# Linear attention with an MLP: where the second token tile's keys and queries stand in a planned instruction order

## The chip, the cores and the metric

The kernel runs on one core of one Trainium2 chip. Its time is the device time of one execution in microseconds (us), given as the median of several runs. The engines are named as in the profile: PE (TensorE, its matmuls; PEld its weight loads), DVE (VectorE), ACT (ScalarE), POOL (GpSimd) and SP (SyncE, whose queue issues every DMA here).

## The reference, cut to what matters

For 8 batches, 8 heads, 576 tokens and a head size of 64, queries and keys are scaled, projected by `omega` to 128 features, shifted by a maximum and exponentiated. Keys and values are summed into a state for each batch and head, queries read it, and the result goes through a layer norm and an MLP of width 2048.

```python
def phi(x):
    proj = np.einsum('bhsd,md->bhsm', x, omega)
    sq = np.sum(x * x, axis=-1, keepdims=True) / 2.0
    h = proj - sq
    h = h - np.max(h, axis=-1, keepdims=True)
    return np.exp(h) / np.sqrt(m)
q_p, k_p = (phi(q_s), phi(k_s))
kv = np.einsum('bhsm,bhsd->bhmd', k_p, v)
z = np.sum(k_p, axis=2)
num = np.einsum('bhsm,bhmd->bhsd', q_p, kv)
den = np.einsum('bhsm,bhm->bhs', q_p, z)[..., None] + 1e-06
...
x = (num / den).transpose(0, 2, 1, 3).reshape(B, S, H * D)
xn = (x - mu) / np.sqrt(var + 1e-06) * g_ln
out = x + np.maximum(xn @ w_ch1, 0.0) @ w_ch2
```

The term `sq` falls out against the maximum, so the kernel never computes it. Here `q` is drawn 4.742 times as large as `k`.

## The kernel before

**Tiles of tokens.** The 4608 tokens are 9 tiles of 512. A tile is 2 query blocks of 256, or 4 chunks of 128. The MLP takes tile after tile (`gen_mlp`): for each of 16 slices f of the hidden width, `mm1(t, f)` is 12 matmuls of 512 columns (L797 to L799: 4 slices of the model width, each with a high and a low part of the weights and of the data) and `mm2(t, f)` 12 more (L830 to L832). `mm2(t, f)` stands behind `mm1(t, f + 1)`. `mm1(t, f)` waits for the group of four first-layer weights that holds f (`w(1, 4*(f//4)+k)`), `mm2(t, f)` for `w(2, f)`.

**Weights.** The 32 weight parts come as 64-bit numbers. `gen_w` loads each one with a 512 KB DMA (L343), turns it into 32-bit numbers with steps on DVE and ACT (L352 to L368), and splits it into a high and a low part. The last step is L379 for first-layer weights and L385 for second-layer ones. At most 3 conversions are open at a time (`turn["w"]`), each with one of 14 `wide` buffers.

**Keys.** `gen_keys` goes through batches b and chunks c of 128 tokens; a batch has 4, and one chunk more holds the remainders of two batches. `gen_k` loads keys and values (L426, L427), projects the keys with 8 unsplit matmuls on 64-row tiles (L514; the trace shows 16 records for them), takes maxima on DVE (L445), exponentiates on ACT (L451), sums into the state on PE (`sums`, L483) and adds it up on DVE (`keep`, L499).

**Queries.** There are two ways. `gen_q`, used for the first tile (`blk < T // QB`, blocks 0 and 1), loads `qT` (L544) and projects it unsplit with 4 matmuls of 256 columns on 64-row tiles (L554; 8 records), two heads side by side. `gen_q2`, used for every other block, loads `qD` (L575), in which each head's numbers stand twice on the partitions, rounds it on ACT (L580), subtracts on DVE to get the low part (L582), and projects with two matmuls of 512 columns against a high and a low `omega` (L589, L590). A block takes 2 calls of `gen_q` or 4 of `gen_q2`. Then `features` copies from PSUM (L230 or L232), takes the maximum over partitions on POOL (L611), subtracts on DVE (L614) and exponentiates on ACT (L617).

**From queries to the MLP.** `gen_x` multiplies the query features of a chunk with the state (L680), divides on DVE (L691 to L695) and takes mean and variance (L713, L715). `gen_rs` makes the reciprocal root for a block (L726 to L738). `gen_xnT` normalizes (L756) and transposes on PE (L770); ACT and DVE write the two parts of `xnT` (L774, L776). There is one `xnT` buffer: the next tile's is written after the last `mm1` of the tile before.

**PSUM.** Of 8 banks, the MLP has 6 once it runs (`mlp_on`); keys, queries, products and transposes share the other two (`at_now`).

**The order.** All instructions are put in order beforehand by a planner in Python (`Plan`), which keeps a clock per engine and a cost per step (the numbers in `us(...)`, `act`, `dve`). Of the steps that can start on an engine it takes the one with the lowest `rank`; MLP steps have the rank `LAST`, so they fill what is left. A `yield wait(...)` or a turn only shapes this order. In the program that comes out, an instruction waits for the data and buffers it uses, and each engine and the SP queue work in the planned order. Ranks before:

- weights: first layer -12 to -10.5 for f below 4, then f - 13.5; second layer f - 10;
- key chunk c of batch 1: 2 + 2c; queries of blocks 2 and 3: 10 and 14; their products and statistics 6 to 8 above;
- `GATE_K`, `GATE_Q`: keys of batch 1 and later enter the plan once `w(2, 5)` is converted, queries of block 2 and later once `w(2, 6)` is.

Tile 1 (the second tile, tokens 512 to 1023) needs the state of batches 0 and 1, so the four chunks of batch 1, and query blocks 2 and 3.

Of the kernel before, what the change touches and what calls it, by code (L numbers as in the profile page):

```python
# [19 lines left out]
PE, ACT, DVE, POOL, SP = "PE", "ACT", "DVE", "POOL", "SP"  # L20
# [15 lines left out]
T = 512  # L36
# [3 lines left out]
QB = 256  # L40
# [28 lines left out]
class Plan:  # L69
# [73 lines left out]
    def free(self, *names):  # L143
        for n in names:
            assert n not in self.places, n
            self.places[n] = self.cur.seen()
            self.cur.holds -= n[0] == "b" and 0 < self.cur.holds
            self.wake(lambda w: w[0] == "get" and n in w[1])

    def done(self, key):  # L150
        self.made[key] = self.cur.seen()
        self.wake(lambda w: w == ("wait", key))
# [38 lines left out]
def favor_ffn(ctx, tc, kT, kTr, vF, vR, qT, qD, omT, gT, w1, w2, out):  # L191
# [21 lines left out]
    def f32(ap):  # L213
        return ap.bitcast(F32)
# [4 lines left out]
    def dve(n, k=1, c=0.065):  # L219
        return "run", {DVE: k * (c + 0.00105 * n)}  # L220

    def us(eng, t):
        return "run", {eng: t}

    def dma(n):
        return "run", {SP: n * 4e-6 / 0.36}
# [13 lines left out]
    def wait(*key):  # L240
        return "wait", key
# [4 lines left out]
    def tile_of(tag, shape, dtype=F32, pool=None):  # L246
        pool = pool or (wp if tag[1].isdigit() and tag[0] == "w" else small if tag[0:2] in ("kv", "mb", "st") or tag[0] == "v" else sb)
        return pool.tile(shape, dtype, tag=tag, name=tag, bufs=1)
# [6 lines left out]
    def bank(tag, n=512):  # L255
        return tile_of(tag, [P, 512], F32, ps)[:, 0:n]
# [10 lines left out]
    mlp_on = []  # L267

    def at_now():
        return b_at if mlp_on else banks  # L270
# [152 lines left out]
    def gen_k(b, c, kraw, v, early, t_v, n_kp):  # L423
# [19 lines left out]
        def side(s, t_b, pk):  # L443
            yield dve(4 * M)
            nc.vector.tensor_reduce(  # L445
                out=mb[:, 4 * s : 4 * s + 4], in_=pk, axis=AX.X, op=ALU.max, negate=True
            )
            yield act(M, 4, 0.142)
            for i in range(4):
                j = 4 * s + i  # L450
                nc.scalar.activation(  # L451
                    out=kp[:, j], in_=pk[:, i], func=AF.Exp, scale=1.0, bias=mb[:, j : j + 1]
                )
            free(t_b)
            done(("kp", b, c, s))
# [50 lines left out]
        plan.add(rank, values())  # L506
        if TILED:
            t_b = yield "get", at_now(), 2
            yield us(PE, 0.9)
            pk = [bank(x).rearrange("p (a b) -> p a b", b=M) for x in t_b]  # L510
            for p in range(NP):
                for h in range(2):
                    a = slice(h * D, (h + 1) * D)
                    nc.tensor.matmul(pk[h][:, p], kraw[a, p], om[a], start=True, stop=True)  # L514
            for s in range(2):
                plan.add(rank, side(s, t_b[s], pk[s]))
        else:
            for s in range(2):
                t_b = yield "get", at_now()
                yield us(PE, 0.87)  # L520
                pk = bank(t_b).rearrange("p (a b) -> p a b", b=M)
                for p in range(2):
                    nc.tensor.matmul(
                        pk[:, 2 * p : 2 * p + 2], kraw[:, 2 * s + p], om, start=True, stop=True
                    )
                plan.add(rank, side(s, t_b, pk))
# [10 lines left out]
    def gen_q(blk, j):  # L537
        rank = plan.cur.rank
        first = n_first if blk < T // QB else ()
        q_turn = () if first else ((yield "get", turn["q"]),)  # L540
        t_q = yield "get", first + n_big
        qraw = tile_of(t_q, [P, 2, QB])
        yield dma(P * 2 * QB)
        nc.sync.dma_start(qraw, qT[blk, j])  # L544
        yield wait("om")

        if TILED:
            t_b = yield "get", at_now(), 2
            yield us(PE, 0.87)
            pq = [bank(x) for x in t_b]  # L550
            for p in range(2):
                for h in range(2):
                    a = slice(h * D, (h + 1) * D)
                    nc.tensor.matmul(pq[h][:, p * QB : (p + 1) * QB], om[a], qraw[a, p], start=True, stop=True)  # L554
            for s in range(2):
                plan.add(rank, features(blk, j, s, t_b[s], pq[s]))
        else:
            for s in range(2):
                t_b = yield "get", at_now()
                yield us(PE, 0.87)  # L560
                pq = bank(t_b)
                for h in range(2):
                    nc.tensor.matmul(pq[:, h * QB : (h + 1) * QB], om[:, h], qraw[:, s], start=True, stop=True)
                plan.add(rank, features(blk, j, s, t_b, pq))
        free(t_q, *q_turn)
# [3 lines left out]
    def gen_q2(blk, j, s):  # L569
        rank = plan.cur.rank  # L570
        q_turn = yield "get", turn["q"]
        t_q = yield "get", n_big
        qraw = tile_of(t_q, [P, 2 * QB])
        yield dma(P * 2 * QB)
        nc.sync.dma_start(qraw, qD[blk, j, s].rearrange("p a b -> p (a b)"))  # L575
        yield wait("om2")
        t_s = yield "get", n_big
        qs = tile_of(t_s, [P, 2 * QB], F32R)
        yield act(2 * QB)
        nc.scalar.copy(out=qs, in_=qraw)  # L580
        yield us(DVE, 0.85)
        nc.vector.tensor_tensor(out=qs[D:P], in0=qraw[D:P], in1=f32(qs[D:P]), op=ALU.subtract)  # L582
        free(t_q, q_turn)
        t_b = yield "get", at_now()

        plan.cur.after = max(plan.cur.after, plan.cur.end + LATE)
        yield us(PE, 0.46)
        pq = bank(t_b)
        nc.tensor.matmul(pq, om_hi, qs, start=True, stop=False)  # L589
        nc.tensor.matmul(pq, om_lo, qs, start=False, stop=True)  # L590
        free(t_s)
        yield from features(blk, j, s, t_b, pq)

    def gen_om2():
        yield dve(M)
        nc.vector.tensor_copy(om_hi, om)
        yield dve(M)
        nc.vector.tensor_tensor(out=om_lo, in0=om, in1=f32(om_hi), op=ALU.subtract)
        done(("om2",))

    def features(blk, j, s, t_b, pq):
        t_c = yield "get", n_big
        qc = tile_of(t_c, [P, 2 * QB])
        eng = yield "run", {ACT: 0.48, DVE: 0.62} if blk >= T // QB else {ACT: 0.58}
        copy(eng, qc, pq)
        free(t_b)
        mx_turn = yield "get", turn["mx"]
        t_m = yield "get", n_big
        mx = tile_of(t_m, [P, 2 * QB])
        yield us(POOL, 1.9)  # L610
        nc.gpsimd.partition_all_reduce(mx, qc, P, bass_isa.ReduceOp.max)  # L611
        done(("mx", blk, j, s))
        yield us(DVE, 0.95 if blk >= T // QB else 0.6)
        nc.vector.tensor_tensor(out=qc, in0=qc, in1=mx, op=ALU.subtract)  # L614
        free(t_m, mx_turn)
        yield act(2 * QB)
        nc.scalar.activation(out=qc, in_=qc, func=AF.Exp)  # L617
        phis[blk, j, s] = t_c, qc.rearrange("p (a b) -> p a b", b=QB)
        done(("phi", blk, j, s))
# [6 lines left out]
    def gen_queries():  # L626
        for blk in range(NB):
            if blk == T // QB:
                yield wait("w", 2, GATE_Q)
                plan.add(plan.cur.rank, gen_om2())  # L630
            plan.cur.rank = NS * (blk * QB // T) + RQ + 4 * (blk % 2) - (7 if blk < T // QB else 0)
            b_turn = yield "get", turn["blk"]
            plan.add(plan.cur.rank, gen_block(blk, b_turn))

    def gen_block(blk, b_turn):
        rank = plan.cur.rank
        for j in range(2):
            if blk < T // QB:
                plan.add(rank, gen_q(blk, j))
            else:  # L640
                for s in range(2):
                    plan.add(rank, gen_q2(blk, j, s))
        t_st = yield "get", n_st
        st = tile_of(t_st, [P, 64])
        for i in range(2):
            plan.add(rank + 6 + 2 * i, gen_x(2 * blk + i, t_st, st))
        plan.add(rank + 8, gen_rs(blk, t_st, st))
        for j in range(2):
            for s in range(2):
                yield wait("phi", blk, j, s)  # L650
        yield wait("num", 2 * blk)
        yield wait("num", 2 * blk + 1)
        free(*(phis[blk, j, s][0] for j in range(2) for s in range(2)), b_turn)
# [241 lines left out]
FIRST = 4  # L895
N_BIG = 14
EARLY, BEFORE = 1, ("x", 3)
GATE_K, GATE_Q = 5, 6
LATE = 1.0
WARM, COLD = 0.0, 5.0  # L900
RW, RS = -10, 0.5
RK, RQ = -30, -22


# [37 lines left out]
```

## Time and profile before

| what | value |
|---|---|
| time, median of 3 runs | 1023.02 us (1022.56 to 1023.74) |
| the profiled execution's own time | 1024.08 us |
| its span, first to last instruction | 1022.3 us |
| busy: DVE, ACT, POOL | 500.2, 351.2, 135.3 us |
| mean granted TensorE clock | 0.992 |
| MLP matmuls | 6 groups of 576, mean 390 to 403 ns each |
| first `mm1` of tile 0, of tile 1, of tile 2 begins | 50.76, 175.81, 305.35 us |
| DMA | 64.19 MB, mean 63 GB/s |

A matmul's duration in the profile holds its whole passage through the array; matmuls follow each other more closely than that, so the pace is read from the starts. Windows of the profile count the busy time of each engine between two times; a timeline shows instructions in order, merged when they are alike, with the engine's idle time and the releaser in brackets.

### The profile page before, as it was taken

How to read it: one execution, taken by the hardware profiler on the slowest of the kernel's cores; microseconds unless marked ns; L12 is line 12 of the kernel's file. 1: busy time of each engine (PE TensorE's matmuls, PEld its weight loads, DVE VectorE, ACT ScalarE, POOL GpSimd, SP SyncE). 2: the span in 40 equal slices, each digit the busy share in tenths (PEclk: the TensorE clock that was granted, in tenths of full speed). 3: DMA queues.
4: the chain of work that ended last, by engine and by line, in shares of the span. 5: the costliest groups of instructions: out<-in, count | busy, mean ns of one | idle time of the engine just before them, and what ended most of it. 6: DMA issues, size and time to landing. Idle time of an engine off the chain costs nothing.

```text
span 1022.3 us, 16484 instructions
## 1 busy us (share of the span) xinstructions
PE 1009.1 (99%) x6778; PEld 818.1 (80%) x6778; DVE 500.2 (49%) x1057; ACT 351.2 (34%) x798; POOL 135.3 (13%) x80
## 2 busy tenths in 40 slices
PE   9999997999999999999999999999999999999998
PEld 7888775878778877887888778888888888888886
DVE  6999848537456532574137532661375134113112
ACT  6689743524533522253114421331133111111100
POOL 5000322203202300050002200140022000000000
PEclk9999996999999999999999999999999999999999
DMA  9553313121222210310013100300030010001001
GB/s 351 214 186 140 105 63 111 45 74 63 63 73 85 63 53 1 125 63 22 1 68 119 32 12 1 105 20 1 10 115 1 1 42 1 1 1 43 1 1 41
DMA packets 30315, 64.19 MB, mean 63 GB/s; under 512 B 3488, under 2 KB 3616, under 8 KB 30240
## 3 DMA queue, kind: packets, MB, share of 16 engines
q1 hardware_dynamic: 30240, 63.14, 18.2%
q8 instruction: 53, 0.87, 0.4%
q14 instruction: 22, 0.18, 0.1%
HBM read 53.69 MB, written 9.44 MB: 62 GB/s over the span
## 4 chain that ended last, share of the span: by engine, by line
PE 93%; DVE 3%; DMA 2%; SPq 0%; issue 0%; ACT 0%; DVEq 0%
PE b L830 14%; PE b L797 14%; PE b L799 13%; PE b L798 13%; PE b L831 13%; PE b L832 13%; PE b L514 3%; PE b L483 3%; PE b L680 3%; DMA w<-w 2%; PE b L770 1%; PE b L589 1%; PE b L590 1%; DMA w<-vF 1%; DVE x L841 1%
## 5 line engine op out<-in xcount | busy, mean ns | idle before, releaser
L810 DVE SCALAR_TENSOR_TENSOR hid<-b,hid 128x512 fp32r<-128x512 f32 x144 | 99.4, 690 | 371.8 <-ACT hid L808 371.4
L808 ACT ACTIVATE hid<-b 128x512 fp32r<-128x512 f32 x144 | 86.2, 598 | 434.6 <-PE b L799 433.7
L830 PE MATMUL b<-w,hid 128*128 128x512 f32 x576 | 232.3, 403 | 0.0
L797 PE MATMUL b<-xnT,w 128*128 128x512 f32 x576 | 229.7, 399 | 0.8 <-ACT xnT L774 0.8
L799 PE MATMUL b<-xnT,w 128*128 128x512 f32 x576 | 224.8, 390 | 0.1
L798 PE MATMUL b<-xnT,w 128*128 128x512 f32 x576 | 224.9, 390 | 0.0
L831 PE MATMUL b<-w,hid 128*128 128x512 f32 x576 | 224.8, 390 | 0.0
L832 PE MATMUL b<-w,hid 128*128 128x512 f32 x576 | 224.8, 390 | 0.0
L611 POOL PARTITION_ALL_REDUCE wide<-wide x72 | 134.2, 1893 | 644.1 <-ACT wide L230 589.4
L797 PEld LDWEIGHTS b<-xnT,w 128*128 128x128 f32 x576 | 108.3, 188 | 25.9 <-ACT xnT L774 1.2
L830 PEld LDWEIGHTS b<-w,hid 128*128 128x128 f32 x576 | 108.1, 188 | 25.0
L799 PEld LDWEIGHTS b<-xnT,w 128*128 128x128 f32 x576 | 108.4, 188 | 23.8 <-DVE xnT L776 0.9
L832 PEld LDWEIGHTS b<-w,hid 128*128 128x128 f32 x576 | 108.1, 188 | 23.2
L798 PEld LDWEIGHTS b<-xnT,w 128*128 128x128 f32 x576 | 108.5, 188 | 21.2
L831 PEld LDWEIGHTS b<-w,hid 128*128 128x128 f32 x576 | 108.3, 188 | 20.1
L451 ACT ACTIVATE kp<-b,mb 128x128 f32<-128x128 f32 x272 | 75.1, 385 | 58.9 <-DVE mb L445 58.6
L445 DVE TENSOR_REDUCE mb<-b 128x4 f32<-128x512 f32 x72 | 46.8, 684 | 38.7 <-PE b L514 38.6
L614 DVE TENSOR_TENSOR wide<-wide,wide 128x512 f32<-128x512 f32 x72 | 62.8, 875 | 6.0 <-POOL wide L611 5.5
L617 ACT ACTIVATE wide<-wide 128x512 f32<-128x512 f32 x72 | 45.5, 636 | 42.4 <-DVE wide L614 40.1
L582 DVE TENSOR_TENSOR wide<-wide,wide 64x512 fp32r<-64x512 f32 x64 | 51.5, 806 | 10.1 <-ACT wide L580 8.3
L230 ACT COPY wide<-b 128x512 f32<-128x512 f32 x58 | 33.3, 592 | 54.1 <-PE b L590 49.8
L680 PEld LDWEIGHTS b<-kv,wide 128*64 128x64 f32 (+1 forms) x1088 | 40.7, 140 | 12.1 <-issue 8.1
(70 smaller groups left out, 796.1 us busy)
## 6 DMA issues: line engine op xcount, KB each, us to landing
w<-w SPq DMA_DIRECT2D x32, 512.0 KB, 8.5
wide<-qD SPq DMA_DIRECT2D x64, 256.0 KB, 2.9
out<-x SPq DMA_DIRECT2D x36, 256.0 KB, 2.0
v<-vF SPq DMA_DIRECT2D x28, 260.0 KB, 2.9
wide<-kT SPq DMA_DIRECT2D x28, 256.0 KB, 2.8
w<-vF SPq DMA_DIRECT2D x4, 260.0 KB, 4.9
v<-vR SPq DMA_DIRECT2D x4, 260.0 KB, 4.1
w<-kT SPq DMA_DIRECT2D x4, 256.0 KB, 5.1
```

The source lines that it names most:

```text
L451: nc.scalar.activation(out=kp[:, j], in_=pk[:, i], func=AF.Exp, scale=1.0, bias=mb[:, j : j + 1])
L611: nc.gpsimd.partition_all_reduce(mx, qc, P, bass_isa.ReduceOp.max)
L614: nc.vector.tensor_tensor(out=qc, in0=qc, in1=mx, op=ALU.subtract)
L680: nc.tensor.matmul(pn[a:z, i], phi(blk, h, slice(cols + a, cols + z)), kvs[b][1][:, h], start=True, stop=True)
L797: nc.tensor.matmul(ph, w[:, 0, cs], xnT[:, 0, k], start=(k == 0), stop=False)
L798: nc.tensor.matmul(ph, w[:, 1, cs], xnT[:, 0, k], start=False, stop=False)
L799: nc.tensor.matmul(ph, w[:, 0, cs], xnT[:, 1, k], start=False, stop=(k == NK - 1))
L808: nc.scalar.activation(out=hl[:, 0], in_=ph, func=AF.Relu)
L810: nc.vector.scalar_tensor_tensor(out=hl[:, 1], in0=ph, scalar=0.0, in1=f32(hl[:, 0]), op0=ALU.max, op1=ALU.subtract)
L830: nc.tensor.matmul(accs[i], hl[:, 0, cs], w[:, 0], start=(f == 0), stop=False)
L831: nc.tensor.matmul(accs[i], hl[:, 0, cs], w[:, 1], start=False, stop=False)
L832: nc.tensor.matmul(accs[i], hl[:, 1, cs], w[:, 0], start=False, stop=(f == NF - 1))
```

## The change

Tile 1's queries (blocks 2 and 3) go through `gen_q` instead of `gen_q2` (`WHOLE = 4`), so `qT` holds four blocks and the high and low `omega` are made when block 4 is reached. `GATE_K` and `GATE_Q` fall from 5 and 6 to 3 and 4. The step of the weights' ranks doubles (`RS`), and `RK` and `RQ` fall by 6. The planner's cost of an unsplit projection on 64-row tiles is 1.15 us while the MLP runs, where it was 0.9 for keys and 0.87 for queries.

```diff
@@ gen_k
             t_b = yield "get", at_now(), 2
-            yield us(PE, 0.9)
+            yield us(PE, 1.15 if mlp_on else 0.9)
@@ gen_q
             t_b = yield "get", at_now(), 2
-            yield us(PE, 0.87)
+            yield us(PE, 1.15 if mlp_on else 0.87)
@@ gen_queries
             if blk == T // QB:
                 yield wait("w", 2, GATE_Q)
+            if blk == WHOLE:
                 plan.add(plan.cur.rank, gen_om2())
@@ gen_block
-            if blk < T // QB:
+            if blk < WHOLE:
                 plan.add(rank, gen_q(blk, j))
@@ constants
-GATE_K, GATE_Q = 5, 6
+GATE_K, GATE_Q = 3, 4
+WHOLE = 4
-RW, RS = -10, 0.5
-RK, RQ = -30, -22
+RW, RS = -10, 1.0
+RK, RQ = -36, -28
@@ kernel
-    qT = np.ascontiguousarray(q5.transpose(3, 0, 1, 2, 4)[: T // QB])
+    qT = np.ascontiguousarray(q5.transpose(3, 0, 1, 2, 4)[:WHOLE])
```

The ranks that follow from it, beside those of before:

| step | before | after |
|---|---|---|
| first-layer weights 0 to 3 | -12 to -10.5 | -14 to -11 |
| first-layer weights 4, 7, 8, 11, 12, 15 | -9.5, -6.5, -5.5, -2.5, -1.5, 1.5 | -9, -3, -1, 5, 7, 13 |
| second-layer weights 0, 4, 8, 12, 15 | -10, -6, -2, 2, 5 | -10, -2, 6, 14, 20 |
| key chunks 0 to 3 of batch 1 | 2, 4, 6, 8 | -4, -2, 0, 2 |
| queries of blocks 2, 3 | 10, 14 | 4, 8 |
| products of block 2, of block 3 | 16 and 18, 20 and 22 | 10 and 12, 14 and 16 |
| first key chunk of batch 2 | 34 | 28 |

## The prediction

> **What bounds the kernel now.** I read the page first, then windows around the first tile boundary, then PE's timeline there.
>
> ```profile
> span 1022.3 us, 16484 instructions
> PE 1009.1 (99%) x6778; PEld 818.1 (80%) x6778; DVE 500.2 (49%) x1057; ACT 351.2 (34%) x798; POOL 135.3 (13%) x80
> ```
>
> PE bounds the span, so only three things shorten it: an earlier start, less PE work, or fewer places where PE stands. The windows (length; PE, PEld, DVE, ACT, POOL busy; granted clock; DMA) show the place:
>
> ```profile
> 50.70:100.00 49.30, 49.24 (x239) 40.08 (x238) 49.00 (x85) 42.22 (x79) 1.78 (x1) 1.00 0.47 164
> 100.00:150.00 50.00, 50.00 (x384) 39.93 (x383) 35.85 (x66) 31.74 (x72) 13.63 (x7) 1.00 0.28 92
> 150.00:159.20 9.20, 9.19 (x120) 6.83 (x118) 5.36 (x21) 2.30 (x6) 0.00 (x0) 1.00 0.14 54
> 159.20:163.40 4.20, 1.37 (x32) 1.15 (x32) 4.05 (x13) 0.30 (x2) 0.00 (x0) 1.00 0.80 248
> 163.40:180.50 17.10, 12.90 (x46) 8.72 (x47) 14.71 (x29) 8.64 (x18) 7.27 (x4) 0.50 0.29 97
> ```
>
> Up to 159 us PE is full. DVE is full too until 100 us (49.00 of 49.30) and has 14 us free in the next 50. Then comes a hole, with the clock at 0.50 for 17.1 us. PE's timeline (start, length, line):
>
> ```profile
> 158.79 0.40 PE L832 MATMUL b<-w,hid 128*128 128x512 f32 x1
> ...
> 164.47 1.94 PE L770 MATMUL b<-ident,wide 128*128 128x128 f32 x8 [3.39 <-DVE st L693]
> ...
> 173.04 1.94 PE L770 MATMUL b<-ident,wide 128*128 128x128 f32 x8 [1.45 <-DVE wide L756]
> 175.81 0.79 PE L797 MATMUL b<-xnT,w 128*128 128x512 f32 x1 [0.83 <-ACT xnT L774]
> ...
> 177.46 2.08 PE L514 MATMUL b<-om,wide 64*128 64x128 f32 x16
> ...
> 180.48 0.41 PE L799 MATMUL b<-xnT,w 128*128 128x512 f32 x1
> ```
>
> Tile 0's MLP ends at 159.0 and tile 1's begins at 175.81, because its last products, statistics and transposes come one after another with nothing else for PE to do. Other boundaries don't look like this; tile 2 to 3:
>
> ```profile
> 423.17 0.39 PE L832 MATMUL b<-w,hid 128*128 128x512 f32 x1
> 423.40 0.39 PE L797 MATMUL b<-xnT,w 128*128 128x512 f32 x1
> ```
>
> Here the next tile follows at the plain pace, 0.23 us a matmul. So one `xnT` buffer is no hindrance; lateness is.
>
> Why tile 1 is late, from SP's, PE's and DVE's timelines: batch 1's first keys, the matmuls around their projection, the last state addition of batch 1, and tile 1's first products.
>
> ```profile
> 49.33 0.33 SPq L426 DMA_DIRECT2D wide<-kT  x1
> ```
> ```profile
> 79.56 0.39 PE L832 MATMUL b<-w,hid 128*128 128x512 f32 x1
> 79.88 1.16 PE L514 MATMUL b<-om,wide 64*128 64x128 f32 x16
> 80.97 0.50 PE L830 MATMUL b<-w,hid 128*128 128x512 f32 x1
> 81.31 0.39 PE L831 MATMUL b<-w,hid 128*128 128x512 f32 x1
> ```
> ```profile
> 139.07 0.90 DVE L499 TENSOR_TENSOR kv<-b,kv 128x260 f32<-128x260 f32 x2 [1.19 <-PE b L483]
> ```
> ```profile
> 147.09 1.15 PE L680 MATMUL b<-kv,wide 128*64 128x65 f32 x32
> ```
>
> The keys are loaded from 49.33 on, projected only at 79.88, and the last chunk is added at 139.97: 60 us for four chunks, because with ranks 2 to 8 they yield to nearly all weights (up to 1.5 and 5) on a full DVE. The first products (147.09) come 12 us before tile 0 ends.
>
> **The change part by part.**
>
> *The hole.* From 159.02 (158.79 and one pace) to 180.48 pass 21.5 us. At full clock the work in it costs: 32 products 1.2 (147.09), 16 transposes 1.9 (twice 1.94 for 8, at half clock), four pairs L589 and L590 1.8 (8 paces), one key projection 1.3 (below), five MLP matmuls 1.1. That is 7.3, so **14.2 us are lost**, some 4 of them to the half clock. This is all the change can win here.
>
> *The order.* Key chunks go to ranks -4 to 2, among first-layer weights 7 to 10, and queries to 4 and 8. Does tile 1 come early enough, and do the weights still come in time? PE's need is in the L797 windows (16 records are four slices f), the supply in L379's windows below them (each record finishes one first-layer weight; the eight of the first window are weights 0 to 7). Tile 0's MLP itself begins at 50.76:
>
> ```profile
> 50.76 0.48 PE L797 MATMUL b<-xnT,w 128*128 128x512 f32 x1
> ```
>
> ```profile
> 50.70:70.20 19.50, 6.32 (x16) 3.17 (x17) 1.00 0.49 161
> 70.20:94.60 24.40, 6.34 (x16) 3.00 (x17) 1.00 0.52 184
> 94.60:121.70 27.10, 6.46 (x16) 2.99 (x17) 1.00 0.35 118
> ```
> ```profile
> 25.00:67.20 42.20, 6.11 (x8) 1.00 0.56 207
> 67.20:83.90 16.70, 2.97 (x4) 1.00 0.48 161
> 83.90:108.20 24.30, 2.98 (x4) 1.00 0.45 160
> ```
>
> Slices 4, 8 and 12 begin after 70.2, 94.6 and 121.7; their weights are ready by about 67.2, 83.9 and 108.2. The margins are 3, 11 and 13.5 us. Prices for what moves ahead of the last group:
>
> ```profile
> L614 DVE TENSOR_TENSOR wide<-wide,wide 128x512 f32<-128x512 f32 x72 | 62.8, 875 | 6.0 <-POOL wide L611 5.5
> L582 DVE TENSOR_TENSOR wide<-wide,wide 64x512 fp32r<-64x512 f32 x64 | 51.5, 806 | 10.1 <-ACT wide L580 8.3
> L445 DVE TENSOR_REDUCE mb<-b 128x4 f32<-128x512 f32 x72 | 46.8, 684 | 38.7 <-PE b L514 38.6
> L611 POOL PARTITION_ALL_REDUCE wide<-wide x72 | 134.2, 1893 | 644.1 <-ACT wide L230 589.4 <-DVE wide L232 28.5 <-issue 6.3
> ```
>
> On DVE, at most: 8 reductions (5.5), 8 state additions (3.6, at 0.45 from 139.07), 8 subtractions L614 (7.0), and block 2's products, an estimate of 5 from the 4.05 us busy between 159.2 and 163.4. That is 21, against which stands what before ran there already. The group then comes by 129 at the latest, if DVE stays as full. But PE arrives later too. Slices 0 to 11 are 276 MLP matmuls, 62.7 us from 50.8, so 113.5; four key projections (1.29 each, below), four sums and two products (1.2 each, as at 147.09) and four query projections (1.26, below) ahead of slice 12 add 17.4 and give 131. The weights win by 2 us at worst. For slice 4, one chunk's two reductions (1.4) may go ahead while PE gains a projection (1.3): the margin of 3 stays. I take no stall; the bounds are 0 and the slower rival below.
>
> *Tile 1's end.* Is there room on DVE for tile 1 before tile 0's MLP is over? From 100 us on DVE ran 35.9 up to 150, 5.4 up to 159.2, 4.1 and 14.7 in the hole: 60.1, tile 2's first steps included. Eight L582 go (8 x 0.81 = 6.4). Packed from 100 us on, all of it ends by 154, even if no part of it came ahead of 100. PE isn't through with tile 0 before 50.8 + 384 paces (87.2) + the fillers above (17.4) + two more products (2.4) = 158. Tile 1's last step, transposing, waits for `xnT` anyway, and so the boundary should look like 423.17. The bound on what stays is 0 below and the part-closed rival above; I take 0, since DVE's room is the nearest row.
>
> *POOL and ACT.* Eight all-reduces (8 x 1.893 = 15.1 us) move up by some 20 us, into a stretch where POOL was busy 1.78 of 49.30 us; nothing but each other is queued there. ACT was busy 42.22 of 49.30 up to 100 and 31.74 of 50 after; eight L580 copies go from it. What hides the exponentials that move up is that weights can take DVE for a copy, and DVE is full; without that cover they come later by what moves, and the margins of slices 8 and 12 bear it.
>
> *Unsplit queries.* Eight ACT copies, eight L582 and four of eight loads of 256 KB go; all are off the path once the hole is closed. PE pays. The first tile shows the form:
>
> ```profile
> 14.16 1.13 PE L554 MATMUL b<-wide,om 64*128 64x256 f32 x8
> ```
>
> One `gen_q` is 1.13 us busy, a key batch between MLP matmuls 1.16 (79.88). From 79.56 to 81.31, less two paces, that key batch cost 1.29, so `gen_q` costs about 1.26 there; 0.2 of it is the going into and out of the 64-row form (79.88 is 0.09 later than a pace after 79.56, and L831 0.11 later than a pace after 80.97). Four are 5.1 us. The sixteen matmuls of 512 columns that they replace are 3.6 at 0.227. **Plus 1.5 us**; the bounds are 0.6 (no switch) and 2.3 (twice the switch).
>
> The Trainium skill, "TensorEngine Tiling (Array Packing)", section "Tiling Modes", says that changing the tiling mode drains the TensorE. The trace agrees with its 0.2 us a batch. The rule speaks against the change, since L589 and L590 needed no switch; by it alone, with nothing else different, the four batches would cost 0.8 and the sum would be 1009.6 instead of 1010.3.
>
> *Banks.* `gen_q` holds both shared PSUM banks until its two copies are through, where `gen_q2` held one; a key batch, a sum or a product may wait behind it on PE, and MLP matmuls only if the plan puts none in between. I take 0; at worst each of the four calls holds PE for as long as its own batch, 1.3, so 5 us, which the part-closed rival has.
>
> *Loads.* SP issues in the planned order, and a key load that waits for a `wide` buffer holds the weight loads behind it. Before, keys were already loaded 30 us ahead of use (49.33 against 79.88), so moving them up costs nothing while conversions run behind loads; if that cover went, the next conversion would start by a landing later.
>
> *Planner costs, `RK` and `RQ` in later tiles, `om2` at block 4.* Later keys and queries keep their distance to each other and stay above all weights. I take 0, between -1 and +2.
>
> **Sum.** 1022.3 - 14.2 + 1.5 = 1009.6 us span. The profiled execution's own 1024.08 becomes 1011.4; the median of runs is 1.06 below the profiled one: 1023.02 - 12.7 = **1010.3 us**.
>
> **The rivals.**
>
> *The hole closes in part.* Only the gates may bite, if tile 1's steps wait for banks and for PE as before. L385's windows show what they are worth:
>
> ```profile
> 50.70:64.10 13.40, 2.05 (x3) 1.00 0.71 234
> 64.10:73.20 9.10, 1.37 (x2) 1.00 0.19 53
> ```
>
> With `w(2, 0)` converted earlier, `w(2, 3)` is ready by 64.1 and `w(2, 5)` by 73.2: 9 us. Tile 1's chain moved by 9 of the hole's 16.8 us leaves 7.8 with about 4 of work: 4 lost, so 1014 (up to 1016 with more products late). For it: the two shared banks; against it: ranks below half of the weights. Chance 0.17.
>
> *A short hole and the half clock.* Here an idle stretch of 3.39 us (to 164.47) was followed by 17.1 us at 0.50. If the hole that stays is that long, a full PE loses 8.5 more: 1010.3 + 4 + 8.5 = 1023, no change. The Trainium skill, "TensorE: Matmul & The Clock Gate", section "The HAM clock gate", says the clock halves after one idle window of about 3.4 us and returns after a busy one; this trace agrees on the fall, but the half clock lasted five such windows. Chance 0.05.
>
> *Slower: weights late at slice 12.* DVE works in order, and before it had 0.3 us of waiting up to 100. If it now stands for POOL behind each of the eight all-reduces (1.9 each, 15 us), the last first-layer weights come at 138 to 144 against PE's 131. PE idles about 10, the clock falls (8.5), and the gain of 12.7 becomes a loss of 6: 1029. It decides from about 4 us of idle on at `mm1(0, 12)`. For it: the full DVE; against it: L614 waited 6.0 us in total, 72 times. Chance 0.09.
>
> *Better*: small waits at other boundaries go too, 1007. Chance 0.05. The forecast keeps 0.64.
>
> **How the numbers follow.** A difference of 0.2% (2 us) is what a measurement of this kernel can tell. Faster holds the forecast, the part-closed and better cases, 0.86, less a little of it for causes unseen: 0.85. Same is the half-clock case, 0.05; slower 0.10. The range runs from 1007.3 (all bounds low) to 1020, leaving out the slower and the half-clock case.
>
> **What would show it.** Right: L514 of batch 1 begins near 66 instead of 79.88; products before 135; no stretch of clock 0.50 between 150 and 190; L797 of tile 1 within 1 us of tile 0's last L832; 32 more L554 records at about 1.26 us per 8; the 50.8 us start unchanged. Wrong: PE waits for DVE L379 at slices 4 or 12; L582 or L614 idle times of 10 us or more; a hole at 159 to 170 that stays; or a new one at tile 1's end.

## The result, and the profile after

The changed kernel takes 1012.42 us (1011.83 to 1012.84), beside 1023.38 us (1022.56 to 1024.52) for the kernel before in the same comparison: ratio 0.9892, with a 95% interval of 0.9875 to 0.9909. That is faster by 11 us, or 1.1%. The profiled execution took 1012.24 us with a span of 1010.4 us.

The page's first part and the row of the granted clock, then windows of the changed kernel over the stretch that the prediction was about (length; PE, PEld, DVE, ACT, POOL busy; clock; DMA):

```profile
span 1010.4 us, 16487 instructions
...
PE 1004.0 (99%) x6794; PEld 813.7 (81%) x6794; DVE 499.9 (49%) x1054; ACT 343.1 (34%) x785; POOL 137.1 (14%) x80
...
PEclk9999999999999999999999999999999999999999
```
```profile
50.20:100.00 49.80, 49.73 (x340) 39.59 (x339) 49.56 (x94) 39.81 (x86) 0.00 (x0) 1.00 0.42 151
100.00:150.00 50.00, 50.00 (x371) 38.52 (x370) 48.86 (x100) 32.77 (x66) 24.20 (x12) 1.00 0.34 116
150.00:168.90 18.90, 18.90 (x129) 15.19 (x128) 14.86 (x22) 9.88 (x20) 7.65 (x4) 1.00 0.14 51
```

The dip of the clock in the seventh slice is gone; the row of before was

```profile
PEclk9999996999999999999999999999999999999999
```

DVE is now full up to 150 us (48.86 of 50, where it was 35.85), so the work that stood in the hole has moved into DVE's free time, and PE has no gap from 100 to 168.9. PE's timeline at the boundary from tile 0 to tile 1:

```profile
168.52 0.40 PE L833 MATMUL b<-w,hid 128*128 128x512 f32 x1
168.75 0.39 PE L798 MATMUL b<-xnT,w 128*128 128x512 f32 x1
```

The last matmul of tile 0 and the first of tile 1 are one pace apart. What made that possible, in the order of PE (L514 projects a chunk of batch 1's keys, L483 sums it, L681 is the first product of tile 1):

```profile
68.48 1.16 PE L514 MATMUL b<-om,wide 64*128 64x128 f32 x16
73.89 1.16 PE L514 MATMUL b<-om,wide 64*128 64x128 f32 x16
79.97 1.15 PE L483 MATMUL b<-v,kp 128*64 128x65 f32 x32
82.64 1.15 PE L483 MATMUL b<-v,kp 128*64 128x65 f32 x32
86.01 1.16 PE L514 MATMUL b<-om,wide 64*128 64x128 f32 x16
92.13 1.16 PE L514 MATMUL b<-om,wide 64*128 64x128 f32 x16
97.53 1.15 PE L483 MATMUL b<-v,kp 128*64 128x65 f32 x32
100.89 1.15 PE L483 MATMUL b<-v,kp 128*64 128x65 f32 x32
...
120.05 1.15 PE L681 MATMUL b<-kv,wide 128*64 128x65 f32 x32
```

The four chunks take 34 us from the first projection to the last sum instead of 60, all of them ahead of the first query, and the first product comes at 120 instead of 147. Tile 0 begins at 50.25 us instead of 50.76, and from the first matmul of tile 3 on both kernels take 598.9 us to the end.

### The profile page after: what moved, and what is told of

The parts are those of the page before. It is cut to its first block, busy times and chain, and to the rows that moved or that the text cites. A ratio compares the mean times of both kernels' runs of the same rounds, so it can differ in the third digit from the quotient of the medians.

```text
span 1010.4 us, 16487 instructions
## 1 busy us (share of the span) xinstructions
PE 1004.0 (99%) x6794; PEld 813.7 (81%) x6794; DVE 499.9 (49%) x1054; ACT 343.1 (34%) x785; POOL 137.1 (14%) x80
## 4 chain that ended last, share of the span: by engine, by line
PE 94%; DVE 4%; DMA 1%; issue 0%; SPq 0%; ACT 0%; DVEq 0%
PE b L798 14%; PE b L831 14%; PE b L800 13%; PE b L799 13%; PE b L832 13%; PE b L833 13%; PE b L681 3%; PE b L514 3%; PE b L483 3%; PE b L771 1%; PE b L589 1%; PE b L590 1%; DMA w<-w 1%; DMA w<-vF 1%; PE b L554 0%; DVE x L842 0%
## 5 line engine op out<-in xcount | busy, mean ns | idle before, releaser
L798 PE MATMUL b<-xnT,w 128*128 128x512 f32 x576 | 230.2, 400 | 0.0
L798 PEld LDWEIGHTS b<-xnT,w 128*128 128x128 f32 x576 | 108.1, 188 | 25.6 <-issue 0.7
L445 DVE TENSOR_REDUCE mb<-b 128x4 f32<-128x512 f32 x72 | 46.6, 683 | 35.5 <-PE b L514 35.5
L681 PEld LDWEIGHTS b<-kv,wide 128*64 128x64 f32 (+1 forms) x1088 | 40.5, 140 | 11.4 <-issue 8.8
L582 DVE TENSOR_TENSOR wide<-wide,wide 64x512 fp32r<-64x512 f32 x56 | 43.7, 787 | 8.7 <-ACT wide L580 7.2
```

The source lines that it names most:

```text
L681: nc.tensor.matmul(pn[a:z, i], phi(blk, h, slice(cols + a, cols + z)), kvs[b][1][:, h], start=True, stop=True)
L798: nc.tensor.matmul(ph, w[:, 0, cs], xnT[:, 0, k], start=(k == 0), stop=False)
```

## The experiments

Most of these kernels are the changed kernel with a part put back, or the kernel before with a part added; e5, e6 and e10 to e12 try something new. The theory on record was that the new order closes the hole, and that the unsplit queries are only a price on PE (theory A). Its first rival was that the relief of DVE and ACT does it (theory B).

| run | time, us | ratio to before, 95% interval |
|---|---|---|
| e1: changed, queries split | 1026.72 | 1.0033 (1.0023 to 1.0044) |
| e2: before, queries unsplit | 1026.29 | 1.0027 (1.0017 to 1.0038) |
| e3: before, gates | 1022.10 | 0.9987 (0.9978 to 0.9996) |
| e4: before, ranks | 1024.63 | 1.0013 (1.0004 to 1.0022) |
| e5: e1, asking for two banks | 1014.08 | 0.9915 (0.9901 to 0.9929) |
| e6: changed, load put back | 1018.76 | 0.9960 (0.9946 to 0.9974) |
| e7: changed, old gates | 1013.37 | 0.9908 (0.9894 to 0.9922) |
| e8: changed, old ranks | 1022.35 | 0.9992 (0.9982 to 1.0001) |
| e9: changed, old planner costs | 1010.61 | 0.9875 (0.9858 to 0.9891) |
| e10: changed, all queries unsplit | 1023.45 | 0.9998 (0.9988 to 1.0007) |
| e11: queries split, a rule for the banks | 1009.48 | 0.9864 (0.9849 to 0.9879) |
| e12: tile 1 unsplit, the rule | 1012.39 | 0.9894 (0.9879 to 0.9908) |

### The parts alone (e1 to e4)

e1 takes the unsplit queries out of the change:

```diff
-WHOLE = 4
+WHOLE = 2
```

> The changed kernel with its new order (gates, ranks, planner costs), but tile 1's queries split again as before (WHOLE = 2). Theory A, the order alone closes the hole and the unsplit queries only cost PE (four batches at 1.26 to 1.7 us against 3.6 us, so 1.9 us more): 1010.5 us, no half clock between 150 and 190 us, tile 1 following tile 0 at the pace. Theory B, the relief counts (8 copies on ACT and 8 L582, 6.4 us on a DVE that is busy 98.4 of 99.8 us up to 150): the queries come later, the hole returns in part, 1014 to 1020 us with a stretch of half clock.

e2 puts them alone into the kernel before:

```diff
-            if blk < T // QB:
+            if blk < WHOLE:
...
+WHOLE = 4
```

> The kernel before with one part of the change: tile 1's queries unsplit (WHOLE = 4); gates, ranks and planner costs as before. Theory A: the hole stays, since keys still stand behind the weights; PE pays up to 1.9 us, part of it inside the hole: 1022 to 1025 us, a half clock of about 17 us after 160. Theory B: tile 1 comes earlier by the 6.4 us that DVE saves: 1015 to 1019 us.

e3 and e4 put in the gates alone and the ranks alone:

```diff
-GATE_K, GATE_Q = 5, 6
+GATE_K, GATE_Q = 3, 4
```

> The kernel before with the gates alone at 3 and 4. If the gates bind (the part-closed rival of the prediction), tile 1's first key projection moves from 79.9 to about 71 and the hole loses up to 9 us: 1013 to 1017 us. If ranks decide (keys at 2 to 8 still yield to almost all weights): the first projection may move, the last state addition stays near 140, 1021 to 1024 us.

```diff
-RW, RS = -10, 0.5
-RK, RQ = -30, -22
+RW, RS = -10, 1.0
+RK, RQ = -36, -28
```

> The kernel before with the ranks alone (weights with step 1, keys and queries 6 lower); gates at 5 and 6, queries split. If ranks decide and the order is enough: hole closed, 1010 to 1013 us, last state addition of batch 1 near 112. If the gates are needed too: first projection at about 79 as before, and a hole that stays by 3 to 8 us: 1014 to 1020 us.

No part gives the gain: unsplit queries alone and ranks alone are slower than the kernel before, and the gates alone win 0.13%. Theory A falls with e1 (1010.5 expected, 1026.7 measured). For e1 theory B named the right direction, though not the size, but e2 speaks against it: the same relief without the order wins nothing. e2 came 1.3 us above theory A's range and e4 above both of its own; only e3 fell into an expected one (the ranks decide). The parts need each other. What e1 looks like on PE, in the same stretch as above (L589 is a split query):

```profile
68.88 1.16 PE L514 MATMUL b<-om,wide 64*128 64x128 f32 x16
74.96 1.16 PE L514 MATMUL b<-om,wide 64*128 64x128 f32 x16
80.36 1.15 PE L483 MATMUL b<-v,kp 128*64 128x65 f32 x32
83.62 0.39 PE L589 MATMUL b<-wide,om_hi 128*128 128x512 f32 x1
86.80 0.39 PE L589 MATMUL b<-wide,om_hi 128*128 128x512 f32 x1
88.61 0.39 PE L589 MATMUL b<-wide,om_hi 128*128 128x512 f32 x1
90.52 1.15 PE L483 MATMUL b<-v,kp 128*64 128x65 f32 x32
94.53 0.47 PE L589 MATMUL b<-wide,om_hi 128*128 128x512 f32 x1
97.23 1.16 PE L514 MATMUL b<-om,wide 64*128 64x128 f32 x16
103.31 1.50 PE L514 MATMUL b<-om,wide 64*128 64x128 f32 x16
```

The first two chunks are projected as early as in the changed kernel. Then four queries of rank 4 pass keys of ranks -2, 0 and 2, and the third projection comes at 97.23 instead of 86.01. That isn't a question of DVE: it is how the planner hands out the two shared PSUM banks. A key projection, a sum and a product ask for both at once, a split query for one. When one bank comes free, the step with the lowest rank is asked first, can't do with one, and the split query behind it takes it. The unsplit query asks for two like all others. I call this theory C. The planner's own record of e1 shows it (step, rank, banks asked, in the order in which they were granted, from the first key chunk on):

```
gen_k    -4   2   (projection, chunk 0)
gen_k    -2   2   (projection, chunk 1)
gen_k    -4   2   (sum, chunk 0)
gen_q2    4   1
gen_q2    4   1
gen_q2    4   1
gen_k    -2   2   (sum, chunk 1)
gen_q2    4   1
gen_k     0   2   (projection, chunk 2)
gen_k     2   2   (projection, chunk 3)
```

At the boundary of e1 the same two banks hurt once more:

```profile
169.79 0.65 PE L514 MATMUL b<-om,wide 64*128 64x128 f32 x2 [0.37 <-ACT wide L230]
170.80 2.07 PE L514 MATMUL b<-om,wide 64*128 64x128 f32 x14 [0.35 <-ACT wide L230]
177.67 2.15 PE L771 MATMUL b<-ident,wide 128*128 128x128 f32 x8 [4.80 <-ACT kp L451]
```

A key chunk of tile 2 has slipped in and holds both banks until ACT has exponentiated it; tile 1's last transposes wait 4.8 us for that.

### Banks or relief (e5, e6)

e5 leaves e1's work and load alone and changes only what a split query of tile 1 asks for:

```diff
-        t_b = yield "get", at_now()
+        if blk < 2 * (T // QB):
+            t_b, other = yield "get", at_now(), 2
+            free(other)
+        else:
+            t_b = yield "get", at_now()
```

> The run with the new order and split queries (1026.7 us) with one thing different: for tile 1 each split query asks the plan for both shared banks at once and gives one back straight away, so that it can't slip in on a single free bank ahead of a key that waits for two. Work, copies on ACT and L582 are as in that run. Theory C, banks: the split queries lost because they took single banks past keys of a lower rank; now the four key chunks go first (last state addition near 103 instead of 123), the hole closes, and PE saves the 1.9 us of the unsplit form: 1010 to 1013 us. Theory B, relief of DVE and ACT: the load is the same, so the hole stays, 1020 to 1027 us.

e6 keeps the unsplit queries and puts the relieved load back:

```diff
+        if blk >= T // QB:
+            for s in range(2):
+                t_s = yield "get", n_big
+                qs = tile_of(t_s, [P, 2 * QB], F32R)
+                flat = qraw.rearrange("p a b -> p (a b)")
+                yield act(2 * QB)
+                nc.scalar.copy(out=qs, in_=flat)
+                yield us(DVE, 0.85)
+                nc.vector.tensor_tensor(out=qs[D:P], in0=flat[D:P], in1=f32(qs[D:P]), op=ALU.subtract)
+                free(t_s)
         t_b = yield "get", at_now(), 2
```

> The changed kernel with the relief undone: each of tile 1's unsplit queries first runs two copies on ACT and two half-tile subtractions on DVE whose results nothing reads (8 and 8 in all, as many as L580 and L582 were). Theory C: keys still go first, the hole stays closed, 1012 to 1014 us. Theory B: the 6.4 us of DVE and 5 us of ACT are back, so the hole comes back, 1018 to 1027 us.

e5 measured 1014.08, 1 us above the range that theory C had given: 12.6 us of the 14.3 between e1 and the changed kernel come from the order of the banks, with the split work unchanged. Its keys run as in the changed kernel, and queries only behind them:

```profile
85.45 1.16 PE L514 MATMUL b<-om,wide 64*128 64x128 f32 x16
90.89 1.16 PE L514 MATMUL b<-om,wide 64*128 64x128 f32 x16
95.61 1.15 PE L483 MATMUL b<-v,kp 128*64 128x65 f32 x32
98.96 1.15 PE L483 MATMUL b<-v,kp 128*64 128x65 f32 x32
102.23 0.39 PE L593 MATMUL b<-wide,om_hi 128*128 128x512 f32 x1
```

So theory C holds for the larger part. e6 took 1018.76 us, 6.3 us more than the changed kernel. C had expected 1012 to 1014, B 1018 and more, so by its time it lies at the lower edge of B. But its trace shows the banks again (L564 is the unsplit query here, L781 the transposes):

```profile
114.19 1.16 PE L514 MATMUL b<-om,wide 64*128 64x128 f32 x16
133.19 1.14 PE L564 MATMUL b<-wide,om 64*128 64x256 f32 x8
138.50 1.13 PE L564 MATMUL b<-wide,om 64*128 64x256 f32 x8
...
169.05 2.23 PE L781 MATMUL b<-ident,wide 128*128 128x128 f32 x8 [3.09 <-ACT kp L451]
```

The two queries of block 3 come at 133.19 and 138.50; in the changed kernel they came at 111.57 and 115.58. That is over 20 us later, where at most 6.4 us of DVE work were put back, and DVE isn't full: from 100 to 150 us it is busy for 40.09 us, against 48.86 in the changed kernel. e6's load stands in series ahead of the projection. So block 3 isn't asking yet when the banks come free, and the first key chunk of batch 2 (114.19) takes both. It keeps them until its maxima (L445, at 128.71, behind weight steps) and exponentials are done. At the boundary the next key chunk does the same to tile 1's last transposes. So e6 is no exact inverse of the relief, and it doesn't show that the relief matters; e5, which carries the whole split load, is only 1.7 us above the changed kernel.

### Gates, ranks, costs (e7 to e9)

e7, e8 and e9 each take one other part out of the change:

```diff
-GATE_K, GATE_Q = 3, 4
+GATE_K, GATE_Q = 5, 6
```

> The changed kernel with the gates back at 5 and 6. If the gates matter beside the ranks, tile 1 comes some 9 us later; there are 20 us between its last statistics and the end of tile 0's MLP, so the hole stays closed and the time at 1012 to 1014 us either way; 1018 or more would say that keys and weights fall out of step.

```diff
-RW, RS = -10, 1.0
-RK, RQ = -36, -28
+RW, RS = -10, 0.5
+RK, RQ = -30, -22
```

> The changed kernel with RS, RK and RQ as before (gates at 3 and 4, queries unsplit). If the ranks are what puts tile 1 ahead: the keys yield to the weights again and the queries stand behind them, so the hole returns, 1020 to 1026 us. If the gates with unsplit queries suffice: 1011 to 1015 us.

```diff
-            yield us(PE, 1.15 if mlp_on else 0.9)
+            yield us(PE, 0.9)
...
-            yield us(PE, 1.15 if mlp_on else 0.87)
+            yield us(PE, 0.87)
```

> The changed kernel with the planner's old costs for the unsplit projections (0.9 and 0.87 us where the trace shows 1.26 to 1.3 between MLP matmuls). The planner then thinks each of some 40 batches 0.3 us shorter than it is. If the costs are a detail: 1011 to 1014 us, hole closed. If the plan falls out of step with PE: waits of PE on DVE or ACT at the boundary, the half clock, 1016 us or more.

The gates are worth about 1 us (1013.37 against 1012.42, intervals overlapping). Without the ranks nothing is left (1022.35). Late keys are only part of the reason: in e8 tile 1's products are through at 152.9, before tile 0's MLP ends at 160.9, and PE's longest wait is again that of the last transposes for a key chunk that holds both banks, 4.7 us (4.8 in e1, 3.1 in e6). The ranks and the unsplit queries are the two that need each other. The costs, which look like a correction towards the trace, don't help: with the old ones the time is 1010.61 us, and the span 1008.8 against 1010.4. Part of the difference stands in the changed kernel's timeline at the boundary from tile 1 to tile 2:

```profile
294.97 0.60 PE L771 MATMUL b<-ident,wide 128*128 128x128 f32 x4
295.98 0.63 PE L771 MATMUL b<-ident,wide 128*128 128x128 f32 x4 [0.41 <-DVE xnT L777]
297.08 0.69 PE L483 MATMUL b<-v,kp 128*64 128x65 f32 x16 [0.47 <-DVE xnT L777]
298.00 0.69 PE L483 MATMUL b<-v,kp 128*64 128x65 f32 x16 [0.24 <-DVE xnT L777]
```

A chunk of the next keys stands between the last transposes and tile 2's first matmul and waits itself. The waits shown are 1.1 us; with the old costs one of 0.2 is left at this place, which makes 0.9 of the 1.6 us of span. The rest stays open. I take the gain for chance in the plan, not for a sign that a wrong cost is better; it wasn't tried further.

### The price of the form, and a rule instead of the special case (e10 to e12)

```diff
-WHOLE = 4
+WHOLE = NB
```

> The changed kernel with the unsplit form for every block (WHOLE = 18): 28 more batches of 8 records in place of 28 times four matmuls of 512 columns, in tiles where PE is the only bound. The price of the form by itself: at 1.26 against 0.91 us each, 9.9 us more, 1022 us; without any cost of going into and out of the 64-row form (1.06 against 0.91), 4.2 us more, 1016.6 us; if the load that DVE and ACT are spared counts in later tiles too, less than that.

1023.45 us are 11.0 more than the changed kernel for 28 more batches: 0.39 us each, against an expected 0.35. So the form costs what the prediction read from the start of the trace, going into and out of it included, where PE is the bound. DVE's relief in later tiles shows no gain.

The last two kernels put the rule into the planner that e5 suggests, for all tiles, and lower the queries' rank by 3 more:

```diff
+        if kind == "get" and what == self.shared and any(
+            p.want[0] == "get" and p.want[1] == what and p.key < part.key for p in self.blocked
+        ):
+            self.blocked.append(part)
+            return None
         if kind == "get":
...
-RK, RQ = -36, -28
+RK, RQ = -36, -31
```

with `plan.shared = b_at`, and `WHOLE = 2` in e11, `WHOLE = 4` and gates of 2 and 3 in e12.

> Queries of all tiles after the first split again (WHOLE = 2), the new gates and ranks (queries 3 lower still, RQ = -31), and a rule in the planner in place of the special case: while a step of a lower rank waits for the two shared banks, no step of a higher rank takes one. Theory C (bank order decides, the unsplit form only costs PE): hole closed, 1010 to 1013 us, at or below the changed kernel. If relief is needed besides: a short hole, half clock in some runs, 1013 to 1018 us.

> The same rule with tile 1's queries unsplit (WHOLE = 4), gates at 2 and 3, RQ = -31. If order and relief both count, this has both: 1010 to 1012 us, the smallest time of all; if the rule adds nothing once tile 1's queries ask for two banks, the changed kernel's 1012.4 us within 1.

e11 is the fastest kernel of the study: 1009.48 us (1009.07 to 1009.79), 2.9 us under the changed kernel, with the split queries of before. Each of the two was timed beside its own runs of the kernel before, and their ratios' intervals just overlap (0.9849 to 0.9879, 0.9875 to 0.9909), but no run of the one reaches a run of the other. Its boundary is closed, too:

```profile
163.49 0.39 PE L840 MATMUL b<-w,hid 128*128 128x512 f32 x1
163.71 0.39 PE L805 MATMUL b<-xnT,w 128*128 128x512 f32 x1
```

e12 doesn't add the relief to that: 1012.39, the changed kernel's time, and 2.9 us over e11. So once the banks go by rank, the unsplit form looks like what theory A had called it, a price on PE. By the sum below 1.9 us are the form's own cost; e12 also has lower gates than e11, so the rest stays open. Rule and rank were changed together in e11; which of them brought it from e5's 1014.1 to 1009.5 stays open.

## Why the prediction was right, and where it wasn't

The forecast was 1010.3 us in a range of 1007.3 to 1020; 1012.4 lies in it. By its steps:

*The hole.* Right in place and size. The prediction had 14.2 us lost between 159.02 and 180.48, and that PE runs through if tile 1 comes in time. It does, and no half clock is left there. (Its split of the loss was off: by its own windows PE is idle for 7.0 of the 14.2 us, so the half clock took some 7, not 4.) The signs that it named came too: first key projection at 68.48 ("near 66"), products from 120.05 ("before 135").

*The weights.* Right: no slice waits. First-layer weights 12 to 15 were put at 129 us at the latest against a need at 131. L379's windows and L798's (16 records are four slices) show 115.2 against 133.3:

```profile
90.00:115.20 25.20, 2.98 (x4) 1.00 0.47 172
```
```profile
101.90:133.30 31.40, 6.83 (x16) 3.12 (x17) 1.00 0.35 121
```

*The price of the unsplit queries*, 1.5 us, was a little small. Between MLP matmuls three of the four batches cost the forecast 1.26:

```profile
103.92 0.39 PE L800 MATMUL b<-xnT,w 128*128 128x512 f32 x1
104.24 1.14 PE L554 MATMUL b<-wide,om 64*128 64x256 f32 x8
105.30 0.50 PE L798 MATMUL b<-xnT,w 128*128 128x512 f32 x1
105.64 0.40 PE L799 MATMUL b<-xnT,w 128*128 128x512 f32 x1
```

(103.92 to 105.64 less two paces of 0.23.) The fourth takes 1.7, so the sum is 5.5 against 3.6, or 1.9. (Four times 1.26 are 5.0, not 5.1, so the forecast's own numbers give 1.4.)

*Zero at the other boundaries* was nearly right. At tile 1's end PE waits for 1.1 us (the four rows from 294.97), but the kernel before waited there too:

```profile
304.73 0.69 PE L483 MATMUL b<-v,kp 128*64 128x65 f32 x16 [0.86 <-DVE v L440]
```

So 0.3 us came on top.

*The 2.1 us between forecast and result.* The span was forecast at 1009.6 and is 1010.4, 0.8 us more. The queries add 0.4 and the boundary 0.3, the earlier start takes 0.5 away; the 0.6 us that remain aren't explained. The rest of the 2.1 us is the forecast's last step, from the profiled execution to the median of the runs. It took the median 1.06 us below the profiled execution, as in the kernel before; here it is 0.18 us above (1012.42 against 1012.24). That step carried over the scatter of three runs, not a property of the kernel.

*POOL.* Tile 1's eight all-reduces run from 106 to 127 us now, not in the stretch up to 100 us whose free time the prediction gave them (POOL is busy for 0.00 us there). PE has no gap in either.

*Unsplit queries, "all off the path once the hole is closed"*, and *Banks* were wrong as reasons. The first took the order for the cause of the closed hole and the queries for a bystander; e1 shows that without them the same order is 3.5 us slower than the kernel before. The second saw that `gen_q` takes both banks where `gen_q2` took one, and put that down as a cost of 0 to 5 us. It was the gain: e5 gets 12.6 us over e1 by nothing else. That the forecast came out right all the same was luck in this part, since the form stood in the change for another reason. The prediction looked at what a step costs while it holds a bank and not at who passes whom when one comes free. The trace of before showed the sign: two split queries stand between the second key projection (88.00) and the first chunk's sum (103.15), though their rank is 10 and the keys' 2 to 8.

```profile
96.71 0.39 PE L589 MATMUL b<-wide,om_hi 128*128 128x512 f32 x1
101.24 0.39 PE L589 MATMUL b<-wide,om_hi 128*128 128x512 f32 x1
```

In the plan of the kernel before, seven of tile 1's eight split queries get their bank while a key step of a lower rank waits for two. "They yield to nearly all weights on a full DVE" was only half the reason.

*The part-closed rival* didn't come about, and its price was wrong: it held the gates alone to be worth 9 us of the hole, but alone they win 1.1 us (e3), and their absence costs about 1 (e7). What it named in its favour, the two shared banks, was the right place to look. The *slower* rival, weights late at slice 12, never showed: in e1, e2 and e4, which are slower than the kernel before, no wait of PE for a weight is listed.

## What to carry to other kernels

When a list scheduler hands out a small pool and some steps ask for two places where others ask for one, those that ask for one can pass those that ask for two, whatever the ranks say: look in the trace for less urgent work between the parts of more urgent work, and make the pool go by rank. Test each part of a combined change alone and left out; here each of the two needed parts alone was worth nothing or less. And a change can win by a side effect of the part that looks like its price.

## What the runs showed of the hardware

The half clock comes and goes in steps of about 3.4 us: it lasted 17.1 us in the kernel before, five such steps, and 6.9 and 3.4 us in the rows below. In the run with unsplit queries alone, windows along the hole show it fall twice, with a full-speed stretch of one step between:

```profile
166.00:172.90 6.90, 5.61 (x15) 2.91 (x13) 6.50 (x13) 4.49 (x10) 3.14 (x2) 0.51 0.12 38
172.90:176.30 3.40, 1.22 (x9) 0.98 (x10) 3.02 (x5) 1.94 (x5) 1.91 (x2) 1.00 0.12 31
176.30:179.70 3.40, 3.40 (x19) 2.35 (x19) 3.27 (x5) 2.01 (x4) 2.17 (x2) 0.50 0.77 224
```

A stretch in which PE was busy for 1.22 of 3.40 us is followed by one at half speed, though PE is full in it. The Trainium skill, "TensorE: Matmul & The Clock Gate", section "The HAM clock gate", says that the clock falls to half after at least one idle window of about 3.4 us and returns after a busy one. The length of the steps agrees. But the stretch before the second fall wasn't idle: 1.22 us of work in 3.40 didn't keep the clock up.

In e5 the same program took 1012.2 and 1012.8 us in two executions with a mean clock of 1.000 and 1014.1 to 1015.4 in three with 0.996 to 0.998. The one execution with a trace, at 1.000, has waits of PE of 0.47, 1.06 and 0.72 us within 3.6 us at its boundary. That waits like these let the clock fall in the slower executions is a guess, since none of those has a trace.
